# Batch 0 of a sparse-attention kernel with a feed-forward stage: zero products in TensorE's waits, block sums of v as f32 products, another order of the start, an earlier load of w_in

## The chip, the core and the metric

The kernel runs on one core of a Trainium2 chip. The metric is the device time of one execution in microseconds (us), the median of ten runs. The engines are named as the profile names them: PE is TensorE (its weight loads, which overlap products, are PEld), DVE is VectorE, ACT is ScalarE, POOL is GpSimd and SP is SyncE. Each engine works through its own queue in order.

## What is computed

```python
# q, k, v: (4 batches, 8 heads, 768 rows, 64); block 32, window 16
k_sum = k.reshape(B, H, nb, block, D).max(axis=3)
v_sum = v.reshape(B, H, nb, block, D).mean(axis=3)
scores_l = scale * q @ k.T                      # kept where |i - j| < 16
scores_s = scale * q @ k_sum.T + log(block)     # 24 blocks
a = softmax(concat([scores_l, scores_s]))
attn = a @ concat([v, v_sum])
x = attn as (3072 tokens, 512)
h = x @ w_in                                    # 512 x 2048
g = h * clip(h + 3, 0, 6) / 6
out = g @ w_out                                 # 2048 x 512
```

The excerpt shortens the reference to its formulas. Attention makes x, and a feed-forward stage with a hard-swish makes the output of x.

## The kernel before, in words

Heads are taken in pairs, four pairs p in a batch, and each batch is cut in two halves of 384 rows. So there are eight tiles of x, each with four pairs. A tile goes through F1 (hidden products `hp`, 16 groups of 128 columns, four products each, then `r` on ACT and `g` on DVE) and F2 (products `op` with `w_out`, copied to `ot` and stored).

The attention of batch 0 comes first, in an order written out by hand for PE, ACT and DVE (lines 480 to 508). POOL's queue is by hand for the whole kernel. For a pair the steps are:

- `K(0,p)`: sixteen transposes of k into `tp` (L297). ACT copies the lower half of the partitions into `kbd`, DVE the upper half (L306). DVE takes the block maximum `red` (L310) and writes `kst` (L317).
- `Tq(0,p,0)`: sixteen transposes of the first 480 rows of q (L336), which ACT copies into `qT` (L337).
- `S_first(p)`: seven score products in two groups (L345), the exponential on ACT (L348), and the mask on DVE (L349), into `at`.
- `v_first(p)`: `vsum0` (L253 to 267) and `vcast` (L245 to 248). `vcast` writes f32 v to bf16 `vbd`, half on ACT and half on DVE. In `vsum0` the indicator `ind` (128 x 32) sums blocks of 32 rows by an f32 product, for two pairs together. ACT copies the sums out (L263), and DMAs rearrange them into `vs96`, 96 rows of 64 (L266).
- `to_vst(g)`: DVE multiplies these sums by a head mask into `vst` of two pairs (L232).
- `Ss(0,g,0)`: block scores of two pairs (L355), exponential into `asum` (L358).
- `AV(0,p,0)`: products `num` (L381, L383) and `den` (L387 to L397), then on ACT a logarithm and an exponential (L399, L400), and x = num times that on DVE (L401).

v is loaded in f32 by eight DMAs on SP (`load_vf`); k and q come by POOL's queue. Loads of the weights (`load_weights`: w_in in four parts with the late rows of q between, then w_out in four) stand behind `hold_loads`: POOL copies one element of the rearranged sums of pairs 2 and 3, which makes POOL wait for them. w_in part 0 serves hidden groups 0 to 3.

After the hand-made start, the list at the end of the function interleaves F1, F2 and the attention of later batches by slots; a scheduler sets PE's, ACT's and DVE's order there. The remaining rows of batch 0's first half of q (`Tq(0,p,1)`, 288 rows) are transposed from slot 2 on.

PSUM banks in use are two each of `ps_h`, `ps_o`, `ps_s`, and `num` and `den` of `ps_n`.

Of the kernel before, what the change touches and what calls it, by code (L numbers as in the profile page):

```python
# [9 lines left out]
F32 = mybir.dt.float32  # L10
BF16 = mybir.dt.bfloat16
# [5 lines left out]
D = 64  # L17
BLK = 32
KB = 64
HALO = 15  # L20
# [12 lines left out]
def kernel(  # L33
# [145 lines left out]
    def hold_loads(src):  # L179

        nc.gpsimd.tensor_copy(pace[0:src.shape[0], 0:1], src)
# [8 lines left out]
                            channel_multiplier=-1, pattern=[[NB, 4], [0, D]])  # L190
    hmv = [hm4[:, 2 * par:2 * par + 2] for par in range(2)]
    osum = [osum4[:, 2 * par:2 * par + 2] for par in range(2)]
    obd = const.tile([128, 2, D], BF16, tag="obd", name="obd")
    hmk = const.tile([128, 2, NB], BF16, tag="hmk", name="hmk")
    half_c = const.tile([128, 1], F32, tag="half", name="half_c")
    zero = const.tile([128, 1], F32, tag="zero", name="zero")
    nc.vector.memset(zero[:], 0.0)

    def zero_off_diagonal(eng, t):
        w = t.rearrange("p n c -> p (n c)").bitcast(F32).rearrange("p (n c) -> p n c", c=64)  # L200
        for r, c in ((slice(0, 64), slice(32, 64)), (slice(64, 128), slice(0, 32))):
            if eng is nc.scalar:
                eng.copy(w[r, :, c], zero[r].unsqueeze(2).to_broadcast([64, NK, 32]))
            else:
                eng.memset(w[r, :, c], 0.0)


    ind = const.tile([128, 32], F32, tag="ind", name="ind")
    nc.vector.memset(ind[:], 0.0)
    for i in range(4):  # L210
        nc.vector.memset(ind[32 * i:32 * i + 32, 8 * i:8 * i + 1], 1.0)
    for p in range(NP):
        zero_off_diagonal(nc.vector if p < 2 else nc.scalar, kbd[p][:])
    for p in range(2):
# [15 lines left out]
    def to_vst(g, a):  # L230
        for par in range(2):
            nc.vector.tensor_tensor(vst[2 * g + par][:], a.unsqueeze(1).to_broadcast([RS, 2, D]), hmv[par],  # L232
                                    op=ALU.mult)
# [11 lines left out]
    def vcast(p):  # L245
        for j in range(2):
            rows = slice(64 * j, 64 * j + 64)
            (nc.vector.tensor_copy if j else nc.scalar.copy)(vbd[p][rows, :, rows], vf[p][rows])


    vps, vs96 = {}, {}

    def vsum0(p):  # L253
        g, par = p // 2, p % 2
        if par == 0:
            vps[g] = ps_n.tile([128, NK, D // 2], F32, tag=("num", "den")[g], name="vps")
        for h in range(2):
            c = 2 * h + par
            nc.tensor.matmul(vps[g][32 * c:32 * c + 32], ind[:], vf[p][:, :, h * (D // 2):(h + 1) * (D // 2)],  # L259
                             start=True, stop=True)  # L260
        if par == 1:
            a = ld.tile([128, NK, D // 2], F32, tag="vr", name="vs8", bufs=2)
            nc.scalar.copy(a[:], vps[g][:])  # L263
            vs96[g] = work.tile([RS, D], F32, tag="vs96", name="vs96")
            for h in range(2):
                (nc.sync if g == 1 and h == 0 else nc.gpsimd).dma_start(  # L266
                    out=vs96[g][:, h * (D // 2):(h + 1) * (D // 2)], in_=a[64 * h:64 * h + 64:8])


    asum = {}  # L270
# [50 lines left out]
            nc.vector.tensor_tensor(o, red[:].unsqueeze(1).to_broadcast([128, 2, NB]), hmk[:], op=ALU.mult)  # L321

    def Tq(b, p, part=None):
        pool, tag = (ps_h, "h") if b == 0 else (ps_s, "s")
        tp = pool.tile([128, S], BF16, tag=tag, name="tp")
        t, i = qb_t[b, p, part]
        if b >= NLONG:
            for s in range(NT):
                nc.tensor.transpose(tp[:, s * 128:(s + 1) * 128], t[:, s].rearrange("p h d -> p (h d)"), ident[:])
            nc.vector.tensor_copy(qT[p][:, PAD:PAD + S], tp[:])  # L330
            return
        lo, hi, n = cut(part)
        r = (hi - lo) // n
        for s in range(n):
            for j in range(2):
                nc.tensor.transpose(tp[64 * j:64 * j + 64, s * r:(s + 1) * r], t[:, 2 * i + j, s], ident[0:r, 0:r])  # L336
        nc.scalar.copy(qT[p][:, PAD + lo:PAD + hi].rearrange("p (c s) -> p c s", s=n),  # L337
                       tp[:, 0:hi - lo].rearrange("p (s c) -> p c s", s=n))
# [12 lines left out]
    def Ss(b, g, half):  # L351
        sp = ps_s.tile([128, 512], F32, tag="s", name="ss")
        for par in range(2):
            p = 2 * g + par
            nc.tensor.matmul(sp[0:RS, 0:HALF], kst[p][:], qT[p][:, PAD + half * HALF:PAD + (half + 1) * HALF],  # L355
                             start=(par == 0), stop=(par == 1))
        a = work.tile([RS, HALF], BF16, tag="asum", name="asum", bufs=4)
        nc.scalar.activation(a[:], sp[0:RS, 0:HALF], AF.Exp, scale=scl)  # L358
        asum[b, g, half] = a
# [8 lines left out]
        return res  # L368

    xt = {}  # L370

    def AV(b, p, half):
        s = 2 * b + half
        if s not in xt:
            xt[s] = xp.tile([128, NP, HALF], BF16, tag="x", name="x")
        a, asm = at[p], asum[b, p // 2, half]
        alt = b == 0 and p % 2 == half
        pool = ps_o if alt else ps_n
        num = pool.tile([128, HALF], F32, tag="o" if alt else "num", name="num")
        bl = blocks_of(half)  # L380
        nc.tensor.matmul(num[:], vst[p][:].rearrange("p h d -> p (h d)"), asm[:], start=True, stop=False)  # L381
        for i, (t, lo, hi, off) in enumerate(bl):
            nc.tensor.matmul(num[:, lo:hi], vbd[p][:, t], a[:, t, off:off + hi - lo],  # L383
                             start=False, stop=(i == len(bl) - 1))
        den = pool.tile([128, HALF], F32, tag="o" if alt else "den", name="den")
        ones = obd[:].rearrange("p h d -> p (h d)")
        nc.tensor.matmul(den[:], osum[p % 2].rearrange("p h d -> p (h d)"), asm[:], start=True, stop=False)  # L387
        t0, t1 = (0, NK // 2) if half == 0 else (NK // 2, NK)
        d3 = den[:].rearrange("p (n c) -> p n c", c=KB)
        nc.tensor.matmul(d3, ones, a[:, t0:t1, HALO:HALO + KB], start=False, stop=False)  # L390

        if half == 0:
            nc.tensor.matmul(d3[:, :, KB - HALO:], ones, a[:, 1:7, 0:HALO], start=False, stop=False)
            nc.tensor.matmul(d3[:, 1:, 0:HALO], ones, a[:, 0:5, HALO + KB:], start=False, stop=True)  # L394
        else:
            nc.tensor.matmul(d3[:, 0:5, KB - HALO:], ones, a[:, 7:12, 0:HALO], start=False, stop=False)
            nc.tensor.matmul(d3[:, :, 0:HALO], ones, a[:, 5:11, HALO + KB:], start=False, stop=True)  # L397
        lg = work.tile([128, HALF], F32, tag="lg", name="lg")
        nc.scalar.activation(lg[:], den[:], AF.Ln)  # L399
        nc.scalar.activation(lg[:], lg[:], AF.Exp, scale=-1.0)  # L400
        nc.vector.tensor_tensor(xt[s][:, p], num[:], lg[:], op=ALU.mult)  # L401
# [57 lines left out]
    def load_weights():  # L459
        for c in range(2):  # L460
            load_w_in(c)
        load_q(0, 0, 4, 1)
        for c in range(2, 4):
            load_w_in(c)
        for c in range(4):
            load_w_out(c)

    def S_first(p):
        for lo, hi in ((0, 4), (4, NK0)):
            Sl(0, p, lo, hi)  # L470

    def v_first(p):
        vsum0(p)
        vcast(p)
        if p == NP - 1:
            hold_loads(vs96[1][:, 0:1])
            hold_loads(vs96[1][:, D // 2:D // 2 + 1])
            load_weights()

    zero_rest()  # L480
    K(0, 0)
    Tq(0, 0, 0)
    v_first(0)
    for p in range(2, NP):
        zero_off_diagonal(nc.vector, vbd[p])
    S_first(0)
    v_first(1)
    K(0, 1)
    Tq(0, 1, 0)
    S_first(1)  # L490
    nc.vector.tensor_scalar_mul(osum4[:], hm4[:], float(BLK))
    K(0, 2)
    to_vst(0, vs96[0][:])
    Tq(0, 2, 0)
    Ss(0, 0, 0)
    v_first(2)
    v_first(3)
    AV(0, 0, 0)
    K(0, 3)
    Tq(0, 3, 0)  # L500
    S_first(2)
    AV(0, 1, 0)
    S_first(3)
    Ss(0, 1, 0)
    to_vst(1, vs96[1][:])
    AV(0, 2, 0)
    AV(0, 3, 0)
    start.__exit__(None, None, None)

# [56 lines left out]
                 + [(None, NTILE - 1)])  # L566
    for n, (f1, f2) in enumerate(work_list):
        for i in range(NFT):
            if f1 is not None:
                F1(f1, i, f2 is None)  # L570
            if f2 is not None:
                for j in range(3):
                    F2(f2, 3 * i + j, by_ft=f2 == 0)
            for _, f in sorted(plan.pop(16 * n + i, []), key=lambda e: e[0]):
                f()
# [31 lines left out]
```

## Time and profile before

| | before |
|---|---|
| median of 10 runs (lowest, highest) | 261.31 us (260.85, 262.13) |
| the profiled execution's own time | 261.7 us |
| its span, first to last instruction | 259.8 us |
| PE busy | 241.4 us (93%) |
| ACT busy | 167.9 us (65%) |
| DVE busy | 155.0 us (60%) |
| POOL busy | 67.4 us (26%) |
| granted TensorE clock, mean | 0.999 |

The span leaves out 1.9 us of the execution's time that lie around its instructions. By stretches of the span, PE is busy as follows:

| stretch, us | PE busy, us | share |
|---|---|---|
| 0 to 5.4 | 0.00 | 0% |
| 5.4 to 10.5 | 3.57 | 70% |
| 10.5 to 16 | 3.71 | 67% |
| 16 to 20 | 3.44 | 86% |
| 20 to 23 | 3.00 | 100% |
| 23 to 28.2 | 3.70 | 71% |
| 28.2 to 36.3 | 7.30 | 90% |
| 36.3 to 64 | 27.65 | 100% |
| 64 to 128 | 61.02 | 95% |
| 128 to 240 | 111.83 | 100% |

In rows of the profile, `out<-in` gives what an instruction writes and reads; shapes are partitions x elements; `x16` is a count; what stands after `|` is busy time in us and the mean of one in ns, then the engine's idle time before the group with what ended it. In the timeline, the columns are the start in us, the length of the merged stretch, the engine, the line, the operation, and in brackets the idle time before it. A busy PE includes the tail of a product, so the length of a group of products is a little more than its pace times its count.

### The profile page before, as it was taken

Reading aid. Unit: us, or ns where it says so; the run is one execution under the profiler, and the core shown is the slowest. Engines: PE = TensorE matmul, PEld = TensorE weight load, DVE = VectorE, ACT = ScalarE, POOL = GpSimd, SP = SyncE. Lnnn points to the kernel's source line nnn. Section 1 sums busy time; section 2 is a strip of 40 time slices with the busy share of each in tenths; the row PEclk is TensorE's granted clock in tenths of the full one; section 3 lists DMA queues with packets and bytes.
Section 4 is the critical chain, followed back from the end, with each engine's and each line's share of the span. In section 5 each row is a group of like instructions: output and inputs, shape, how many; then the busy total and the mean of one; then the engine's idle time right before and its main releaser. Section 6 shows DMA issues by size and latency. Waiting matters only on the chain.

```text
span 259.8 us, 5035 instructions
## 1 busy us (share of the span) xinstructions
PE 241.4 (93%) x1952; PEld 139.9 (54%) x1952; DVE 155.0 (60%) x357; ACT 167.9 (65%) x326; POOL 67.4 (26%) x101
## 2 busy tenths in 40 slices
PE   1779789999999999798999999999999999999994
PEld 1336456644555556565555555566655555555553
DVE  4877256632578948999884697658544444444400
ACT  8577469833887878869676657766856655555410
POOL 7316500742991112979430400000000000000000
PEclk9999999999999999999999999999999999999999
DMA  6962999899999186999991551101011111101122
GB/s 127 199 119 37 205 204 201 128 231 212 178 202 119 24 256 78 96 81 194 179 134 40 36 68 42 43 1 43 0 40 43 40 40 43 40 0 42 43 81 81
DMA packets 62847, 25.80 MB, mean 99 GB/s; under 512 B 51280, under 2 KB 58728, under 8 KB 62824
## 3 DMA queue, kind: packets, MB, share of 16 engines
q0 software_dynamic: 52848, 17.61, 58.4%
q1 hardware_dynamic: 9976, 7.88, 9.8%
q8 instruction: 15, 0.25, 0.4%
q14 instruction: 8, 0.07, 0.1%
HBM read 31.98 MB, written 6.29 MB: 147 GB/s over the span
## 4 chain that ended last, share of the span: by engine, by line
PE 75%; DVE 10%; DMA 6%; ACT 4%; issue 2%; SPq 1%; POOL 0%; ACTq 0%
PE op L431 29%; PE hp L414 28%; DMA vf<-in_v_dram 3%; PE num L383 3%; PE sl L345 3%; DVE g L418 2%; DMA win<-in_moe_w_in_dram 2%; PE ss L355 2%; PE num L381 2%; PE den L387 2%; PE den L390 2%; DVE red L312 1%; ACT r L417 1%; PE tp L336 1%; PE vps L259 1%
## 5 line engine op out<-in xcount | busy, mean ns | idle before, releaser
L414 PE MATMUL hp<-x,win 128*128 128x384 bf16 x512 | 105.9, 329 | 2.3 <-DVE g L418 1.5
L417 ACT ACTIVATE r<-hp,half_c 128x384 f32<-128x384 f32 x128 | 73.4, 580 | 45.5 <-PE hp L414 43.4
L418 DVE SCALAR_TENSOR_TENSOR g<-r,hp 128x384 bf16<-128x384 f32 x128 | 69.7, 551 | 51.7 <-ACT r L417 51.4
L431 PE MATMUL op<-wout,g 128*128 128x512 bf16 x368 | 98.3, 379 | 0.0
L414 PEld LDWEIGHTS <-win 128*128 128x128 bf16 x512 | 47.8, 98 | 37.6 <-issue 5.7
L431 PEld LDWEIGHTS <-g 128*128 128x128 bf16 x368 | 35.2, 98 | 30.4 <-issue 0.6
L401 DVE TENSOR_TENSOR x<-num,lg 128x384 bf16<-128x384 f32 x32 | 17.7, 554 | 27.4 <-ACT lg L400 25.7
L399 ACT ACTIVATE lg<-den 128x384 f32<-128x384 f32 x32 | 15.7, 492 | 19.3 <-PE den L394 11.7
L120 POOL DMA_DIRECT2D vbd<-in_v_dram x24 | 18.1, 770 | 35.1 <-PE num L383 24.1
L348 ACT ACTIVATE at<-sl 128x376 bf16<-128x376 f32 (+2 forms) x48 | 22.2, 488 | 4.8 <-PE sl L345 4.7
L349 DVE TENSOR_TENSOR at<-at,mask 128x376 bf16<-128x376 bf16 (+2 forms) x48 | 16.3, 348 | 3.5 <-ACT at L348 3.2
L345 PEld LDWEIGHTS <-kbd 128*128 128x128 bf16 x192 | 12.5, 103 | 9.1 <-DVE kbd L306 3.0
L400 ACT ACTIVATE lg<-lg 128x384 f32<-128x384 f32 x32 | 16.8, 526 | 0.9
L435 ACT COPY ot<-op 128x512 f32<-128x512 f32 x23 | 13.2, 585 | 5.9 <-PE op L431 5.7
L383 PEld LDWEIGHTS <-vbd 128*128 128x128 bf16 x224 | 13.9, 104 | 5.6 <-issue 2.4
L345 PE MATMUL sl<-qT,kbd 128*128 128x94 bf16 x192 | 15.4, 216 | 1.6 <-DVE kbd L306 1.6
L383 PE MATMUL num<-at,vbd 128*128 128x94 bf16 (+2 forms) x224 | 15.1, 208 | 0.0
L113 POOL DMA_DIRECT2D qb<-in_q_dram x16 | 13.6, 880 | 3.7 <-DMA vr<-in_v_dram 1.9
L113 POOL DMA_DIRECT2D kb<-in_k_dram x16 | 13.6, 872 | 0.4 <-PE hp L414 0.4
L381 PE MATMUL num<-asum,vst 96*128 96x384 bf16 x32 | 11.2, 350 | 0.6 <-ACT vs L263 0.6
L390 PE MATMUL den<-at,obd 128*128 128x384 bf16 x32 | 11.4, 357 | 0.0
L387 PE MATMUL den<-asum,osum 96*128 96x384 bf16 x32 | 11.0, 345 | 0.0
(87 smaller groups left out, 215.7 us busy)
## 6 DMA issues: line engine op xcount, KB each, us to landing
out_dram<-ot SPq DMA_DIRECT2D x23, 256.0 KB, 2.0
vr<-in_v_dram POOLq DMA_DIRECT2D x6, 768.0 KB, 9.3
vbd<-in_v_dram POOLq DMA_DIRECT2D x24, 96.0 KB, 4.5
win<-in_moe_w_in_dram POOLq DMA_DIRECT2D x4, 512.0 KB, 9.2
wout<-in_moe_w_out_dram POOLq DMA_DIRECT2D x4, 512.0 KB, 17.5
vf<-in_v_dram SPq DMA_DIRECT2D x8, 192.0 KB, 7.5
kb<-in_k_dram POOLq DMA_DIRECT2D x16, 96.0 KB, 5.1
qb<-in_q_dram POOLq DMA_DIRECT2D x16, 96.0 KB, 5.0
```

The costliest lines, as they stand in the source:

```text
L113: nc.gpsimd.dma_start(out=t[:, :, j], in_=src[b, 2 * p + j].rearrange("(s p) d -> p s d", p=128))
L120: nc.gpsimd.dma_start(out=vall[rows, p, lo:hi, rows], in_=v[b, 2 * p + j].rearrange("(n k) d -> k n d", k=KB)[:, lo:hi])
L345: nc.tensor.matmul(sp[:, i * WIN:(i + 1) * WIN], kbd[p][:, t], qT[p][:, PAD - HALO + t * KB:PAD - HALO + t * KB + WIN], start=True, stop=True)
L348: nc.scalar.activation(a, sp[:, 0:n * WIN].rearrange("p (n c) -> p n c", c=WIN), AF.Exp, scale=scl)
L383: nc.tensor.matmul(num[:, lo:hi], vbd[p][:, t], a[:, t, off:off + hi - lo], start=False, stop=(i == len(bl) - 1))
L390: nc.tensor.matmul(d3, ones, a[:, t0:t1, HALO:HALO + KB], start=False, stop=False)
L400: nc.scalar.activation(lg[:], lg[:], AF.Exp, scale=-1.0)
L401: nc.vector.tensor_tensor(xt[s][:, p], num[:], lg[:], op=ALU.mult)
L414: nc.tensor.matmul(hp[:], w_in_sb[:, kt, ft * 128:(ft + 1) * 128], xt[t][:, kt], start=(kt == 0), stop=(kt == NP - 1))
L417: nc.scalar.activation(r[:], hp[:], AF.Relu, bias=half_c[:], scale=1.0 / 6.0)
L418: last_g[0] = nc.vector.scalar_tensor_tensor(gt[t][:, ft], r[:], 1.0, hp[:], op0=ALU.min, op1=ALU.mult)
L431: nc.tensor.matmul(op[:], gt[t][:, ft, ts * 128:(ts + 1) * 128], w_out_sb[:, ft], start=(ft == 0), stop=(ft == NFT - 1))
```

## The change

1. An all-zero bf16 tile `idle` (128 x 512). Ten products of it into a bank of `ps_n` stand first in PE's queue, and four more between the transposes of k and q of pair 0.
2. `vsum0` sums v in another way: twelve f32 products per pair, one for each 64 rows, with a 96-column slice of a wider indicator. They accumulate over two pairs in a bank of 96 x 64, which `to_vst` reads directly. The copy, the rearranging DMAs and `vs96` go.
3. The order of the start is another one. `K(0,1)` comes before the first scores of pair 0; `K` and `Tq` of pair 3 come before the first outputs; casts of v of pairs 2 and 3 come later.
4. The hold ahead of the weight loads reads `kbd` of pair 2, where it read the sums of pairs 2 and 3.
5. The zeros off the diagonal of `vbd` for pairs 2 and 3 are written by POOL, not by DVE.
6. `AV(0,p,0)` and the transposes of q use other PSUM banks, and F1 of tile 0 is scheduled after the last `den` product of pair 2.

```diff
+    for p in range(2, NP):
+        w = vbd[p].rearrange("p n c -> p (n c)").bitcast(F32).rearrange("p (n c) -> p n c", c=64)
+        nc.gpsimd.memset(w[0:64, :, 32:64], 0.0)
+        nc.gpsimd.memset(w[64:128, :, 0:32], 0.0)
...
+    idle = const.tile([128, 512], BF16, tag="idle", name="idle")
+    nc.vector.memset(idle[:], 0.0)
...
+    def busy(t, n):
+
+        for _ in range(n):
+            nc.tensor.matmul(t[:], idle[:, 0:128], idle[:], start=True, stop=True)
+
+    busy_n = ps_n.tile([128, 512], F32, tag="den", name="busy_n")
+    busy(busy_n, 10)
...
-    ind = const.tile([128, 32], F32, tag="ind", name="ind")
+    ZI = 2 * NB + NK - 1
+    ind = const.tile([128, ZI + RS], F32, tag="ind", name="ind")
...
-            nc.tensor.matmul(vps[g][32 * c:32 * c + 32], ind[:], vf[p][:, :, h * (D // 2):(h + 1) * (D // 2)],
-                             start=True, stop=True)
...
+        for n in range(lo, hi):
+            o = ZI - par * 2 * NB - n
+            nc.tensor.matmul(vps[g][:], ind[:, o:o + RS], vf[p][:, n], start=(par == 0 and n == 0),
+                             stop=(par == 1 and n == NK - 1))
...
     K(0, 0)
+    busy(busy_n, 4)
     Tq(0, 0, 0)
-    v_first(0)
-    for p in range(2, NP):
-        zero_off_diagonal(nc.vector, vbd[p])
+    vsum0(0)
+    vcast(0)
+    K(0, 1)
     S_first(0)
-    v_first(1)
-    K(0, 1)
+    vsum0(1, 0, NK // 2)
     Tq(0, 1, 0)
+    vsum0(1, NK // 2, NK)
+    vcast(1)
+    nc.vector.tensor_scalar_mul(osum4[:], hm4[:], float(BLK))
+    to_vst(0, vps[0][:])
+    K(0, 2)
+    hold_loads(kbd[2][0:64, 0, 0:1])
+    load_weights()
     S_first(1)
-    nc.vector.tensor_scalar_mul(osum4[:], hm4[:], float(BLK))
-    K(0, 2)
-    to_vst(0, vs96[0][:])
     Tq(0, 2, 0)
-    Ss(0, 0, 0)
-    v_first(2)
-    v_first(3)
-    AV(0, 0, 0)
     K(0, 3)
     Tq(0, 3, 0)
+    Ss(0, 0, 0)
+    vsum0(2)
+    vcast(2)
     S_first(2)
-    AV(0, 1, 0)
+    AV(0, 0, 0)
+    vcast(3)
+    vsum0(3)
+    to_vst(1, vps[1][:])
     S_first(3)
     Ss(0, 1, 0)
-    to_vst(1, vs96[1][:])
+    AV(0, 1, 0)
     AV(0, 2, 0)
+    first_x = last_av[0]
     AV(0, 3, 0)
...
-            if f1 is not None:
+            if f1 == 0:
+                with tc.issue_after(first_x.ins):
+                    F1(0, i, True)
+            elif f1 is not None:
                 F1(f1, i, f2 is None)
```

More of the change, by code (lines that the diff above doesn't have):

```diff
@@ L205, in zero_off_diagonal @@
                 eng.memset(w[r, :, c], 0.0)
-    ind = const.tile([128, 32], F32, tag="ind", name="ind")
+    ZI = 2 * NB + NK - 1
+    ind = const.tile([128, ZI + RS], F32, tag="ind", name="ind")
     nc.vector.memset(ind[:], 0.0)
     for i in range(4):
-        nc.vector.memset(ind[32 * i:32 * i + 32, 8 * i:8 * i + 1], 1.0)
+        nc.vector.memset(ind[32 * i:32 * i + 32, ZI + NK * i:ZI + NK * i + 1], 1.0)
     for p in range(NP):
@@ L248, in vcast, with vsum0 @@
             (nc.vector.tensor_copy if j else nc.scalar.copy)(vbd[p][rows, :, rows], vf[p][rows])
-    vps, vs96 = {}, {}
-    def vsum0(p):
+    vps = {}
+    def vsum0(p, lo=0, hi=NK):
         g, par = p // 2, p % 2
[L255 to L259, printed above, removed]
-                             start=True, stop=True)
[L261 to L267, printed above, removed]
+        if par == 0 and lo == 0:
+            vps[g] = ps_n.tile([RS, D], F32, tag=("num", "den")[g], name="vps")
+        for n in range(lo, hi):
+            o = ZI - par * 2 * NB - n
+            nc.tensor.matmul(vps[g][:], ind[:, o:o + RS], vf[p][:, n], start=(par == 0 and n == 0),
+                             stop=(par == 1 and n == NK - 1))
     asum = {}
@@ L323, in Tq @@
     def Tq(b, p, part=None):
-        pool, tag = (ps_h, "h") if b == 0 else (ps_s, "s")
+        pool, tag = (ps_s, "s") if b else (ps_o, "o") if part == 0 else (ps_h, "h")
         tp = pool.tile([128, S], BF16, tag=tag, name="tp")
@@ L370 @@
     xt = {}
+    last_av = [None]
     def AV(b, p, half):
@@ L376, in AV @@
         a, asm = at[p], asum[b, p // 2, half]
-        alt = b == 0 and p % 2 == half
-        pool = ps_o if alt else ps_n
-        num = pool.tile([128, HALF], F32, tag="o" if alt else "num", name="num")
+        pool, tags = (ps_n, ("num", "den")) if b or p == 2 or half and p % 2 == 0 else (ps_h, "hh") if p == 1 and half == 0 else (ps_o, "oo")
+        num = pool.tile([128, HALF], F32, tag=tags[0], name="num")
         bl = blocks_of(half)
@@ L384, in AV @@
                              start=False, stop=(i == len(bl) - 1))
-        den = pool.tile([128, HALF], F32, tag="o" if alt else "den", name="den")
+        den = pool.tile([128, HALF], F32, tag=tags[1], name="den")
         ones = obd[:].rearrange("p h d -> p (h d)")
@@ L393, in AV @@
             nc.tensor.matmul(d3[:, :, KB - HALO:], ones, a[:, 1:7, 0:HALO], start=False, stop=False)
-            nc.tensor.matmul(d3[:, 1:, 0:HALO], ones, a[:, 0:5, HALO + KB:], start=False, stop=True)
+            last_av[0] = nc.tensor.matmul(d3[:, 1:, 0:HALO], ones, a[:, 0:5, HALO + KB:], start=False, stop=True)
         else:
@@ L470, in S_first @@
             Sl(0, p, lo, hi)
[L472 to L478, printed above, removed]
     zero_rest()
     K(0, 0)
+    busy(busy_n, 4)
     Tq(0, 0, 0)
-    v_first(0)
-    for p in range(2, NP):
-        zero_off_diagonal(nc.vector, vbd[p])
+    vsum0(0)
+    vcast(0)
+    K(0, 1)
     S_first(0)
-    v_first(1)
-    K(0, 1)
+    vsum0(1, 0, NK // 2)
     Tq(0, 1, 0)
+    vsum0(1, NK // 2, NK)
[5 more added lines that the diff above has]
+    load_weights()
     S_first(1)
-    nc.vector.tensor_scalar_mul(osum4[:], hm4[:], float(BLK))
-    K(0, 2)
-    to_vst(0, vs96[0][:])
     Tq(0, 2, 0)
-    Ss(0, 0, 0)
-    v_first(2)
-    v_first(3)
-    AV(0, 0, 0)
     K(0, 3)
     Tq(0, 3, 0)
+    Ss(0, 0, 0)
+    vsum0(2)
+    vcast(2)
     S_first(2)
-    AV(0, 1, 0)
+    AV(0, 0, 0)
+    vcast(3)
+    vsum0(3)
+    to_vst(1, vps[1][:])
     S_first(3)
     Ss(0, 1, 0)
-    to_vst(1, vs96[1][:])
+    AV(0, 1, 0)
     AV(0, 2, 0)
+    first_x = last_av[0]
     AV(0, 3, 0)
```

## The prediction, made before the changed kernel ran

> **What bounds the kernel now.** I read four views in this order: the page's shares by engine, the chain of waits over the first 70 us, the timeline of the start, and the groups by shape of the first 36 us. The page puts TensorE (PE) at 93% of the span; from 36.30 us on, PE waits for another engine for 3.4 us in all. What can move is the start, so the question is when the last output tile of batch 0, x of pair 3, is written. From the chain of waits (start, length, what):
>
> ```profile
> 3.00 7.50 DMA vf<-in_v_dram
> ...
> 12.17 0.48 ACT vs L263
> ...
> 20.00 1.87 DMA vs<-vs
> ...
> 22.68 5.50 DMA win<-in_moe_w_in_dram
> 28.18 0.05 issue
> 28.23 1.46 PE hp L414 x4
> 29.69 0.32 PE num L381
> ...
> 35.70 0.56 DVE g L418
> 36.26 0.04 issue
> 36.30 0.43 PE tp L336 x16
> ```
>
> The end is set by v arriving, block sums, a small transfer that rearranges them (vs), a hold that lets w_in go only then (22.68), 5.50 us for w_in part 0, four hidden-layer products, and behind these in PE's queue the outputs (num, den) of pairs 2 and 3. x of pair 3 is written at 34.54; the first later transposes (tp) run 1.76 us after that.
>
> w_in is not late alone. The block sums of pairs 2 and 3 are multiplied out (vst) only at 27.42 to 27.90, so with w_in early and nothing else changed, pair 2 could begin at 27.9 instead of 29.69: 1.8 us. More must come from the engines. The second thing to see is PE's pace:
>
> ```profile
> 32.67 2.87 PE L414 MATMUL hp<-x,win 128*128 128x384 bf16 x12
> ...
> 33.62 0.15 PEld L414 LDWEIGHTS <-win 128*128 128x128 bf16 x1 [0.17 <-issue]
> 33.94 1.20 PEld L414 LDWEIGHTS <-win 128*128 128x128 bf16 x7 [0.17 <-issue]
> ```
>
> Weight loads of one and the same product start 0.32 us apart until 33.94, then 0.17 us apart. The granted clock is 1.00 throughout, so it doesn't show this; durations do. All of PE's work before 33.9 runs at half pace. Third, from the groups by shape (busy us and mean ns of one, then idle before it), the old sums and DVE's load:
>
> ```profile
> L259 PE MATMUL vps<-vf,ind 128*32 128x384 f32 x16 | 4.5, 846 | 0.9 <-DMA vf<-in_v_dram 0.9
> ...
> L306 DVE COPY kbd<-tp 64x768 bf16<-64x768 bf16 x4 | 3.8, 960 | 3.9 <-ACT kbd L306 3.8
> L310 DVE TENSOR_REDUCE red<-tp 128x24 bf16<-128x768 bf16 x4 | 3.8, 958 | 0.1
> ...
> L401 DVE TENSOR_TENSOR x<-num,lg 128x384 bf16<-128x384 f32 x4 | 2.2, 558 | 7.3 <-ACT lg L400 7.3
> ```
>
> DVE (VectorE) is idle 7.3 us before the outputs: it has room now, which the change uses up.
>
> **The change part by part.** DMA landings don't move: issue plus time to landing gives k of pair 1 at 9.7, k of pairs 2/3 at 13.1, q of 2/3 at 14.6, v of pairs 0 to 3 at 7.2, 10.5, 15.7, 17.2.
>
> *Block sums.* Gone: eight products of 384 columns (16 records, 4.5 us), two ACT copies of 0.48, four small transfers (4.3 us landing, three of POOL's issues of 0.61), one hold. Added: 48 f32 products, weights 96 columns, moving 64. The old ones took two records each and 4 records in 1.49 us for two products side by side, so 0.64 us a record for 384 columns, or 0.107 us for 64 at half pace, 0.053 at full. A weight load may hide or not: an f32 load of 32 columns lasted 0.14, so the ends per record are 0.107 to 0.2 slow, 0.053 to 0.13 full. I take 0.15 and 0.08, between: nearest row 0.076 pitch for 94-column bf16 products whose loads hide. That is 96 records: 7.7 us at full pace, 14.4 at half.
>
> *Products of zeros.* 14 products of 512 columns. At 384 columns in 0.32, one costs 0.43 at half pace: ten from 1.1 (after two memsets) to 5.4, where k of pair 0 lands (5.4): hidden. Four more stand before the q transposes of pair 0: 6.1 to 7.8 at half pace, 0.8 us past q's landing at 7.0. Cover: what follows needs k of pair 1 at 9.7. Without cover they cost 0.8.
>
> *Does it warm PE?* Row: PE had no gap from 28.23 to 33.94, so 5.7 us passed before the pace doubled. [...] The trace agrees as far as it can: PE was also busy from 20.0 to 23.77, of which 1.4 us were transposes, and stayed slow. [...] By the row, counting anew after the transposes of pair 0, full pace at 12 to 14: 29.2 to 29.8. I take 8.
>
> *Order.* K(0,1) ahead of the first scores, K and q transposes of pair 3 ahead of the first outputs; zeros of vbd for pairs 2/3 from DVE (4 x 0.378) to POOL, some 0.46 each by hm's memset of 0.31 for 256 columns, 8.9 to 10.8, needed after 17: hidden. DVE's two larger early memsets (0.2) lie in its 2.4 us of idle before 7.17.
>
> *w_in.* The hold now reads kbd of pair 2, which ACT copies after k's landing: 13.1, transposes, ACT's queue, 14.5. So w_in is issued at 15.1 instead of 22.68; its data would flow some 2 us later, when v (17.2) is in. Landing 20.6 to 22. The whole list on POOL moves 7.6 us earlier: the late part of q from 34.1 to 26.5, w_in parts 1 to 3 from 30.7, 36.1, 38.6 to 23.1, 28.5, 31.0; their uses (36.3, 36.8, 41.1, 44.2) move by 7.0 at my forecast, so slack stays. The w_out parts (41.2 to 48.8) have nine us.
>
> *No hidden-layer product before pair 2's outputs*: takes the 1.46 us out of PE's queue there; behind it nothing waits any more for w_in.
>
> **The sum.** With PE fast, DVE becomes the bound. Its first copy for pair 1 can start at about 11.6 (sums of pair 0 to 10.2, k transposes 0.5, ACT copy 0.79). From then without a gap: 0.96 + 0.96 + 0.28 (kbd, red, kst of pair 1), masks 0.57, cast 0.56, osum 0.28, vst 0.48 = 4.1; pair 2: 2.20 + masks 0.57 = 2.8; pair 3: 2.2; cast 0.56, masks 0.57, x of pair 0 0.56, cast 0.56, vst 0.48 = 2.7. Together 11.8, so vst of pairs 2/3 is there at 23.4. Then num and den of pair 2 at full pace (1.0, as they ran from 45.53 to 46.55): 24.5; ACT's logarithm and exponential for pairs 2 and 3, four of 0.52: 26.6; x of pair 3, 0.56: **27.2**. ACT is near its limit too (16.8 us of work from 6.3: 23.1 with no wait), so no much better order hides behind DVE. The same summing of the old queues, at half pace, gives 34.75 where the trace has 34.54, so I trust it to some tenths.
>
> Saved 34.54 - 27.2 = 7.3; then hidden products that must wait for x of pair 3 (its bank is also shared by the second of them) make the handover about 2.1 instead of 1.76: -0.3. All later queues have the same order. So 261.7 (the profiled execution; its span is 259.8) - 7.0 = 254.7. That execution lies 0.4 above the median 261.31: forecast **254.3**.
>
> **Rivals.**
> *Late warming* (full pace at 12 to 14; or the 96 records cost 0.13 each at full pace): x of pair 3 at 29.2 to 31.0, time 256.3 to 258. For it: 5.7 us in the trace and the transposes. Against: PE's queue has almost no gap from 1.1 to 12 now.
> *PE stays slow and the new sums are its bound*: PE's work after 7.8 without sums is 4 x 0.48 + 3 x 0.66 + 4 x 0.55 + 2 x 0.64 + 4 x 1.6 = 13.8, plus 96 records: at 0.15, 14.4, so 36.0, and 2.3 for the last log, exponential and x: 38.3, or 3.8 later than now, **265**; at 0.187 it is 268. It decides above 0.11 a record. For it: all PE work before 33.9 was slow, though often 70 to 86% busy. Against: a PE so bound has no gaps, which is what made it fast at 33.9.
> *The transfers undo it*: w_in's data share the queue with v of pair 3; if v of pairs 2 and 3 land 2 us later, x of pair 3 is at 28.2 (pair 2's sums stand ahead of the first output): 255.4. Speaks against: the 2 us between issue and flow.
>
> **How the numbers follow.** Forecast 0.57; late warming or dear records 0.20; transfers 0.10; slow PE 0.10, of which some ends near no change; the rest 0.03. The best end is DVE starting at 10.6, k-bound: 252.8. The range takes that and late warming's upper part: 252.6 to 258.4. Within 0.2% is what cannot be told from no change. Faster 0.87, same 0.03, slower 0.10.
>
> **What would show it.** Right: weight loads and 128x384 products at the short spacing before 10 us; DVE without gaps from about 12 to 23; vs transfers gone; w_in issued near 15; PE waiting for vst or ACT, not w_in; the first late transposes near 29.3. Wrong: products of zeros but 0.32 spacing after 12; the sums' records above 0.1 at full pace; hp or tp waiting for win or qb after 27; time after 36 us not equal to before's.

## The result, and the profile after

| | before | changed |
|---|---|---|
| median, us | 261.48 (32 runs) | 254.78 (9 runs, 254.29 to 258.73) |
| profiled execution, its time and span | 261.7, 259.8 | 255.62, 253.5 |
| w_in issued | 22.68 | 15.04 |
| vst of pairs 2 and 3 complete | 27.90 | 23.57 |
| x of pair 3 complete | 34.54 | 28.29 |
| first late transposes | 36.30 | 29.93 |

The ratio is 0.9746 (95% interval 0.9731 to 0.976): 6.7 us saved. In a later group of runs the changed kernel took 254.88. Ratios leave out runs more than 1.5% above a kernel's shortest, here one of nine (258.73) and below most runs of one kernel, which are therefore given in full.

The late transposes begin 6.37 us earlier and the span is 6.3 us shorter, so the whole gain is in the start and nothing is given back later. The chain of waits of the changed kernel (start, length, what):

```profile
6.47 10.63 DMA vf<-in_v_dram
17.09 0.14 issue
17.23 2.22 PE vps L274 x24
...
20.61 2.06 PE vps L274 x24
22.67 0.18 PE sl L353 x4
22.88 0.49 ACT at L356
...
23.41 0.48 PE ss L363 x2
23.89 0.17 PE num L389
...
24.79 0.50 ACT lg L407
...
25.74 0.48 ACT lg L407
...
26.67 0.48 ACT lg L407
27.18 0.53 ACT lg L408
27.73 0.57 DVE x L409
28.30 0.04 issue
28.34 0.34 PE hp L422
```

Neither the small transfer nor w_in is in it any more. What is left is v of pair 2, the f32 sums of pairs 2 and 3, the scores behind them, the outputs of pair 1 (num, from 23.89), and then three pairs of logarithms and exponentials on ACT. `vst` is not in it. In the timeline, the rows that answer to PE's pace:

```profile
1.27 4.38 PE L208 MATMUL busy_n<-idle 128*128 128x512 bf16 x10 [1.27 <-DVE zero L203]
...
5.58 0.53 PE L305 MATMUL tp<-ident,kb 96*64 96x96 bf16 x16
...
6.04 1.04 PE L208 MATMUL busy_n<-idle 128*128 128x512 bf16 x4
...
7.83 2.25 PE L274 MATMUL vps<-vf,ind 128*96 128x64 f32 x24
```

The same k transposes in the profile of before:

```profile
5.46 0.85 PE L297 MATMUL tp<-ident,kb 96*64 96x96 bf16 x16 [5.46 <-DMA kb<-in_k_dram]
```

They took 0.85 us there and take 0.53 now, four products of zeros 1.04 instead of 4 x 0.43, and 24 records of the new sums 2.25, so 0.09 each with the tail off. PE is at full pace from 5.6 us on. DVE, in its own timeline, has no gap from 11.44 to 24.04; then it waits for ACT:

```profile
20.24 0.28 DVE L325 TENSOR_TENSOR kst<-red,hmk 128x24 bf16<-128x24 bf16 x2
20.55 0.85 DVE L263 CAST vbd<-vf 64x768 bf16<-64x768 f32 x1
21.42 0.57 DVE L357 TENSOR_TENSOR at<-at,mask 128x376 bf16<-128x376 bf16 x2
21.91 0.55 DVE L409 TENSOR_TENSOR x<-num,lg 128x384 bf16<-128x384 f32 x1
22.49 0.56 DVE L263 CAST vbd<-vf 64x768 bf16<-64x768 f32 x1
23.08 0.49 DVE L247 TENSOR_TENSOR vst<-vps,hm 96x128 bf16<-96x128 f32 x2
...
25.87 0.56 DVE L409 TENSOR_TENSOR x<-num,lg 128x384 bf16<-128x384 f32 x1 [1.82 <-ACT lg L408]
```

### The profile page after: what moved, and what is told of

It is laid out like the page before. It is cut to its first block, busy times and chain, and to the rows that moved or that the text cites. A ratio compares the mean times of both kernels' runs of the same rounds, so it can differ in the third digit from the quotient of the medians.

```text
span 253.5 us, 5214 instructions
## 1 busy us (share of the span) xinstructions
PE 242.9 (96%) x2046; PEld 144.5 (57%) x2046; DVE 154.3 (61%) x354; ACT 166.9 (66%) x324; POOL 67.2 (27%) x101
## 4 chain that ended last, share of the span: by engine, by line
PE 75%; DVE 11%; DMA 5%; ACT 4%; SPq 2%; issue 2%; ACTq 0%
PE op L439 29%; PE hp L422 27%; DMA vf<-in_v_dram 4%; PE num L391 3%; DVE g L426 3%; PE sl L353 3%; SPq L129 2%; PE ss L363 2%; PE num L389 2%; PE den L395 2%; PE vps L274 2%; PE den L398 2%; DVE red L320 2%; ACT r L425 1%; DVE x L409 1%
## 5 line engine op out<-in xcount | busy, mean ns | idle before, releaser
L422 PE MATMUL hp<-x,win 128*128 128x384 bf16 x512 | 104.7, 326 | 1.9 <-DVE g L426 1.5
L439 PEld LDWEIGHTS <-g 128*128 128x128 bf16 x368 | 35.2, 98 | 30.4 <-issue 0.6
L407 ACT ACTIVATE lg<-den 128x384 f32<-128x384 f32 x32 | 15.7, 491 | 14.3 <-PE den L405 7.3
L408 ACT ACTIVATE lg<-lg 128x384 f32<-128x384 f32 x32 | 16.8, 526 | 0.9
L391 PEld LDWEIGHTS <-vbd 128*128 128x128 bf16 x224 | 12.9, 98 | 5.1 <-issue 1.6
L353 PEld LDWEIGHTS <-kbd 128*128 128x128 bf16 x192 | 11.8, 98 | 6.1 <-issue 1.0
L353 PE MATMUL sl<-qT,kbd 128*128 128x94 bf16 x192 | 14.4, 206 | 0.0
L391 PE MATMUL num<-at,vbd 128*128 128x94 bf16 (+2 forms) x224 | 14.1, 199 | 0.0
L398 PE MATMUL den<-at,obd 128*128 128x384 bf16 x32 | 10.7, 333 | 0.0
L389 PE MATMUL num<-asum,vst 96*128 96x384 bf16 x32 | 10.4, 326 | 0.1
L395 PE MATMUL den<-asum,osum 96*128 96x384 bf16 x32 | 10.4, 325 | 0.0
## 6 DMA issues: line engine op xcount, KB each, us to landing
wout<-in_moe_w_out_dram POOLq DMA_DIRECT2D x4, 512.0 KB, 16.8
```

What stands on the lines that cost most here:

```text
L353: nc.tensor.matmul(sp[:, i * WIN:(i + 1) * WIN], kbd[p][:, t], qT[p][:, PAD - HALO + t * KB:PAD - HALO + t * KB + WIN], start=True, stop=True)
L422: nc.tensor.matmul(hp[:], w_in_sb[:, kt, ft * 128:(ft + 1) * 128], xt[t][:, kt], start=(kt == 0), stop=(kt == NP - 1))
L439: nc.tensor.matmul(op[:], gt[t][:, ft, ts * 128:(ts + 1) * 128], w_out_sb[:, ft], start=(ft == 0), stop=(ft == NFT - 1))
```

## The experiments

Times of the kernel before beside them: 261.43, 261.40 and 261.71 in the three groups of runs. "First late tp" is where the transposes of q's late rows begin, as in the table above.

| kernel | median, us | pace of PE | w_in issued | first late tp |
|---|---|---|---|---|
| changed | 254.78 | full from 5.6 | 15.04 | 29.93 |
| changed, no zero products | 263.24 | half until about 29 | 19.79 | 37.72 |
| changed, first ten only (long runs) | 263 | full to 8, half to about 29 | 19.79 | 37.67 |
| changed, narrow f32 fill | 263.98 | half until about 29 | 20.56 | 38.31 |
| before, zero products | 261.66 | full 6 to 13, lost twice | 23.73 | 36.98 |
| before, zero products in the waits too | 260.12 | full from about 7 | 23.25 | 34.92 |
| changed, late w_in | 258.38 | full | 22.59 | 33.03 |
| changed, old sums | 273.57 | full to 15, then lost | 14.66 | 48.19 |
| changed, old sums, late w_in | 266.95 | lost twice | 29.33 | 42.14 |

**Is it the zero products? The changed kernel without them.**

```diff
-    busy(busy_n, 10)
...
-    busy(busy_n, 4)
```

> The changed kernel without its 14 products of zeros. My theory (the fill brings PE to full pace before 6 us): without it PE starts slow, the f32 records of pair 0 cost 0.11 to 0.15 us instead of 0.09, and full pace comes near 12 us at the earliest, from the unbroken sums after the q transposes: x of pair 3 some 2 us later, so 256.5 to 257.5 against 254.8. Rival 1 (the denser new order warms PE by itself, the fill is idle work): 254.8 within 0.4. Rival 2 (nothing else would warm it in the start): PE-bound, 262 or more.

Measured: 263.24 us (ratio 1.0066, 1.0037 to 1.0096). My number was too small by 6 us; rival 2 is right. The timeline:

```profile
7.81 4.10 PE L272 MATMUL vps<-vf,ind 128*96 128x64 f32 x24
11.84 0.85 PE L303 MATMUL tp<-ident,kb 96*64 96x96 bf16 x16
...
21.92 4.00 PE L272 MATMUL vps<-vf,ind 128*96 128x64 f32 x24
...
27.85 2.62 PE L272 MATMUL vps<-vf,ind 128*96 128x64 f32 x24
30.30 0.46 PE L351 MATMUL sl<-qT,kbd 128*128 128x94 bf16 x7
```

PE has no gap from 10 to 29 us, and the sums stay at 0.165 us a record. Two stretches of them last about 4 us unbroken. Full pace comes only within the last 24 records (2.62 us, between the 4.00 of half pace and the 2.22 of full), after the first wide bf16 outputs (26.27 to 27.85). So here being busy in the profile was not enough to raise the pace. With PE slow, k of pair 2 is transposed late too, and w_in goes at 19.79: the pace moves the loads as well.

**Which products raise it? A fill of narrow f32 products.**

```diff
-    idle = const.tile([128, 512], BF16, tag="idle", name="idle")
+    idle = const.tile([128, 96], F32, tag="idle", name="idle")
...
-            nc.tensor.matmul(t[:], idle[:, 0:128], idle[:], start=True, stop=True)
+            nc.tensor.matmul(t[0:96, 0:64], idle[:], idle[:, 0:64], start=True, stop=True)
...
-    busy(busy_n, 10)
+    busy(busy_n, 13)
...
-    busy(busy_n, 4)
+    busy(busy_n, 5)
```

> The changed kernel with its fill made of f32 products of 64 columns with 96-column weights (13 and 5 in place of 10 and 4, about the same 4.3 us at the slow pace, PE just as busy in the profile). Theory (what raises the pace is wide products that keep the array streaming; the narrow f32 ones that ran from 10 to 29 us without the fill did not): as without a fill, 262.5 to 264. Rival (any unbroken 4 us of products raises it, and only the transposes between stood in the way): 254.8 within 0.5.

Measured: 263.98 us (1.0064 to 1.0121), as the theory said. Its timeline:

```profile
1.10 4.42 PE L208 MATMUL busy_n<-idle 128*96 128x64 f32 x26 [1.10 <-DVE zero L203]
5.45 0.85 PE L305 MATMUL tp<-ident,kb 96*64 96x96 bf16 x16
```

PE is as long busy as with the wide fill (4.42 against 4.38 us), and the transposes behind it take 0.85 instead of 0.53. One profile would not settle it: the changed kernel with the first ten only, the next run, comes out short in three executions of ten and long in seven. But all six runs are long (263.35 to 264.51), and so are the ten without a fill (262.54 to 264.29). So between these two fills the kind of product decides. The two fills differ in width, in type, in the columns of their weights and in the number of weight loads; no run separates these.

**Are the four later ones needed?**

```diff
-    busy(busy_n, 4)
```

> The changed kernel without the four later products of zeros. Full pace stood at 5.6 us already, and PE then waits 1.0 us for q of pair 0 instead of filling it. Theory (ten raise the pace, small waits don't lower it): 254.8 within 0.4. Rival (the four are needed, because transposes and narrow f32 products count little): the pace falls back between 8 and 15 us, 258 or more.

Measured: ten runs, three at 254.14 to 254.91 and seven at 262.75 to 263.31. The rival is right seven times in ten. The profiled execution, one of the long ones, by stretches (us, each engine's busy time and count, granted clock, DMA share, GB/s):

```profile
5.40:7.00 1.60, 0.53 (x16) 0.40 (x16) 0.00 (x0) 1.45 (x3) 1.40 (x5) 1.00 1.31 215
7.00:9.00 2.00, 1.45 (x24) 1.41 (x24) 1.75 (x2) 1.13 (x3) 1.74 (x6) 0.77 1.30 197
9.00:11.00 2.00, 2.00 (x15) 2.00 (x15) 1.02 (x4) 0.45 (x1) 1.75 (x4) 0.50 1.23 200
```

Between 5.4 and 7.0 PE does 0.53 us of transposes and nothing else. At 8 the granted clock falls to half (0.50 from 10 to 25), and the sums that follow do not bring it back. Six of the seven long runs have a mean granted clock of 0.96, which is some 21 us at half (an estimate: 0.04 of 261 us, doubled), as in this profile; the seventh reads 0.998, and what happened in it is open. The same kernel comes out 8 us apart from run to run. No short run of it was profiled, so what saved it is not shown.

**The zero products alone, in the old kernel.** The diff adds the tile, the function and both calls of the change.

> The old kernel with the 14 products of zeros only. My theory: PE runs at full pace from 6 us, so the outputs of pairs 2 and 3 take 1.0 us each instead of 1.6, but they still stand behind w_in part 0, which is issued at most 1 us earlier than 22.7: time 258 to 259. Rival (PE falls back to the slow pace in the old order's waits, which are longer): 261.3 within 0.4, with weight loads 0.32 us apart at 30 us. Rival (w_in didn't matter, only the pace did): 255 to 256.

Measured: 261.66 us (0.9979 to 1.0033), no change. My theory is wrong and the first rival right. By stretches:

```profile
10.00:15.00 5.00, 2.30 (x43) 1.42 (x43) 4.28 (x9) 2.45 (x5) 1.22 (x2) 0.77 1.23 212
15.00:20.00 5.00, 5.00 (x52) 2.17 (x51) 4.43 (x14) 3.46 (x7) 0.00 (x0) 0.55 0.39 57
...
25.00:30.00 5.00, 1.10 (x5) 0.40 (x5) 1.62 (x7) 0.71 (x2) 5.00 (x8) 0.64 1.06 160
30.00:35.00 5.00, 4.87 (x35) 3.05 (x34) 0.77 (x2) 2.03 (x4) 0.50 (x1) 0.68 1.25 204
```

PE is busy 2.30 of the 5 us from 10 on, and the clock falls. It recovers near 19.5 (0.55 from 15 to 20, 1.00 from 20 to 25) and is lost again in the wait for w_in (0.64 from 25 to 30):

```profile
29.36 1.46 PE L424 MATMUL hp<-x,win 128*128 128x384 bf16 x4 [3.90 <-DMA win<-in_moe_w_in_dram]
```

**The old kernel with the waits filled too.**

```diff
     Tq(0, 1, 0)
+    busy(ps_o.tile([128, 512], F32, tag="o", name="busy_o"), 8)
...
     Ss(0, 1, 0)
+    busy(ps_o.tile([128, 512], F32, tag="o", name="busy_o"), 14)
```

> The old kernel with the 14 products of zeros and 22 more in the two waits where the pace was lost: 8 behind the q transposes of pair 1 (2 us of wait near 12 us), 14 behind the block scores of pairs 2 and 3 (the wait for w_in near 26 us). Theory 1 (fill alone did nothing because the old order's waits undid it): full pace from 6 us to the end, outputs of pairs 2 and 3 take 1.0 us instead of 1.6, but w_in still lands near 28: 259 to 260. Rival (pace is worth nothing in the old order, w_in and the vs transfers set everything): 261.5 within 0.4. Rival (w_in comes earlier too once PE is fast): below 258.

Measured: 260.12 us (ratio 0.9914 to 0.9975), 0.1 above the range of theory 1. From about 7 us the pace holds (no granted clock under 1.00 to 50 us, and every later product short), `num` and `den` of all four pairs are done at 29.6, and then:

```profile
30.07 2.77 PE L424 MATMUL hp<-x,win 128*128 128x384 bf16 x16 [0.49 <-DMA win<-in_moe_w_in_dram]
34.92 0.43 PE L346 MATMUL tp<-ident,qb 36*64 36x36 bf16 x16 [2.08 <-DMA qb<-in_q_dram]
```

Full pace without the early loads, in the old order, is worth 1.3 us: late q rows, behind w_in in POOL's queue, become the wait.

**The changed kernel with w_in late.**

```diff
-    hold_loads(kbd[2][0:64, 0, 0:1])
-    load_weights()
...
     vcast(3)
+    hold_loads(vbd[3][0:64, 0, 0:1])
+    load_weights()
```

> The changed kernel with the hold on ACT's half of the cast of v of pair 3, so w_in is issued near 22.6 us instead of 15.0. Two questions. Is the early load needed: my theory says that F1 then waits for w_in (28.3) and the first late transposes for the late rows of q (near 33 instead of 29.9): 257.5 to 258.5. Rival (DVE and ACT are the only bound): below 255.5. And why v of pair 2 landed at 17.1 instead of the 15.7 of before: if w_in's early issue takes part of v's transfers, v of pairs 2 and 3 lands near 15.7 and 17.2 again here and x of pair 3 comes up to 1 us earlier than 28.3; if it is not w_in, v lands at 17.1 and 18.1 here too.

Measured: 258.38 us, 3.6 above the changed kernel, as the theory said. F1 waits for w_in, then the transposes for q:

```profile
28.09 2.77 PE L422 MATMUL hp<-x,win 128*128 128x384 bf16 x16 [1.64 <-DMA win<-in_moe_w_in_dram]
...
33.03 0.43 PE L344 MATMUL tp<-ident,qb 36*64 36x36 bf16 x16 [0.59 <-DMA qb<-in_q_dram]
```

The second question: the later transfer for v of pair 2, issued at 6.0 here, took 11.0 us to land (17.0), with w_in still unissued. With w_in at 14.66 (the next run) it landed at 15.7, as before the change. So v lands between 15.7 and 17.1 from one execution to the next, and w_in doesn't set that.

**The new order with the old sums.** Indicator, `vsum0` and `vs96` of the old kernel, the rest as changed.

> The changed kernel with the old block sums (two wide f32 products a pair, ACT copy, rearranging transfers), in the new order, with the fill and the early hold. PE saves some 6 us of the 8.6 us of small f32 products, but vst waits for copies and transfers of 2 to 4.4 us that stand in POOL's queue among the weight loads. My theory (the direct sums matter by cutting these transfers): vst of pairs 2 and 3 comes at 25 or later, 256 to 258. Rival (PE's share of the new sums is a loss of its own): vst at 23.5 or before, S_first of pairs 2 and 3 earlier, 254.5 or less.

Measured: 273.57 us (1.0412 to 1.0481), worse than the theory by far, for a reason that I had named and not priced:

```profile
41.45 0.50 PE L395 MATMUL num<-asum,vst 96*128 96x384 bf16 x1 [15.34 <-DVE vst L246]
```

POOL's half of the sums of pairs 2 and 3 was issued at 24.2 and landed 16.8 us later: it stood behind 8 parts of weights that POOL had issued before it, and the quickest of these transfers in this run took 4.6. To take that away:

```diff
-    hold_loads(kbd[2][0:64, 0, 0:1])
-    load_weights()
...
     vsum0(3)
+    hold_loads(vs96[1][:, 0:1])
+    hold_loads(vs96[1][:, D // 2:D // 2 + 1])
+    load_weights()
```

> The new order and the fill, with the old block sums and the old hold on their transfers. It takes away what spoilt the run with old sums and early w_in, where the vs transfers stood behind the weights for 15 us. Theory: PE has fewer products between 8 and 15 us, loses the pace near 15 again, and w_in is issued near 25: 263 to 265. Rival (the new order is worth it without the new sums): 258 or less.

Measured: 266.95 us (1.0128 to 1.0251), two above the range. Three waits stand out: one for DVE, whose queue waits for the sums of pairs 0 and 1, one for `vst` of pairs 2 and 3, and one for w_in:

```profile
20.16 0.73 PE L359 MATMUL sl<-qT,kbd 128*128 128x94 bf16 x7 [3.31 <-DVE kbd L320]
...
28.93 0.34 PE L395 MATMUL num<-asum,vst 96*128 96x384 bf16 x1 [2.51 <-DVE vst L246]
...
34.84 6.27 PE L428 MATMUL hp<-x,win 128*128 128x384 bf16 x20 [3.77 <-DMA win<-in_moe_w_in_dram]
```

By stretches:

```profile
20.00:25.00 5.00, 4.05 (x30) 2.19 (x31) 4.77 (x12) 3.24 (x8) 0.06 (x1) 0.66 0.00 0
...
30.00:35.00 5.00, 1.23 (x13) 0.76 (x12) 1.14 (x3) 2.03 (x4) 5.00 (x8) 0.54 0.88 135
...
40.00:45.00 5.00, 3.81 (x54) 2.24 (x53) 1.49 (x4) 2.51 (x6) 0.00 (x0) 0.94 1.24 206
```

The pace falls at 20.2, at the end of the first wait, is back at 23.6, falls again at 30.4, between the second wait and the third, and stays at half to 40.6; so the 20 hidden products take 6.27 us. So the new order without the new sums is a loss of 5.5 us. The direct sums do two things for it: they need no transfer, so the weights can go first, and with them PE is busy 4.78 of the 5 us from 10 to 15.

**Is there more in the order?** Two variants beside the changed kernel, on one chip.

> The changed kernel once more, beside the two below on one chip: 254.3 to 255.3, with v of pair 2 landing anywhere from 15.7 to 17.1 us in the profiled execution.

> The changed kernel with the tail of its start in another order: block scores of pairs 0/1 before the q transposes of pair 2, first scores of pair 2 ahead of its sums, those of pair 3 ahead of the first outputs, casts of pair 3 with those of pair 2. In the changed kernel PE waits 0.9 us for v of pair 2 with the scores of pair 2 queued behind, and the outputs of pair 1 start only at 23.7 because the scores of pair 3 stand behind its sums. Theory (v's landing and the sums behind it set x of pair 3): x of pair 3 near 27.5 instead of 28.3, 253.8 to 254.3. Rival (DVE's work alone sets it, vst of pairs 2 and 3 at 23.5 in any order): same as the changed kernel within 0.3.

> The changed kernel with three more products of zeros behind the block scores of pairs 0 and 1, in the 0.9 us that PE waits for v of pair 2. They end before v lands, so nothing should be later: 254.3 to 255.3. If the one run of the changed kernel at 258.7 had lost the pace in that wait, no such run should come here; the rival is that the products run past v's landing when it is early (15.7) and cost up to 0.6.

```diff
# the other order
     S_first(1)
+    Ss(0, 0, 0)
     Tq(0, 2, 0)
     K(0, 3)
     Tq(0, 3, 0)
-    Ss(0, 0, 0)
+    S_first(2)
     vsum0(2)
     vcast(2)
-    S_first(2)
-    AV(0, 0, 0)
     vcast(3)
+    S_first(3)
+    AV(0, 0, 0)
     vsum0(3)
     to_vst(1, vps[1][:])
-    S_first(3)
# more fill
     Ss(0, 0, 0)
+    busy(ps_n.tile([128, 512], F32, tag="den", name="busy_2"), 3)
     vsum0(2)
```

Measured: the changed kernel 254.88, the other order 255.12, more fill 255.48 (0.2 above its range); the intervals of the ratios overlap (0.9716 to 0.9764, 0.9727 to 0.9769, 0.9745 to 0.9802). Neither is an improvement. In the changed kernel's second profile v of pair 2 was not waited for, x of pair 3 stood at 27.72 and the late transposes at 29.34. From the other order's timeline:

```profile
22.89 0.33 PE L389 MATMUL num<-asum,vst 96*128 96x384 bf16 x1
...
23.30 0.47 DVE L247 TENSOR_TENSOR vst<-vps,hm 96x128 bf16<-96x128 f32 x2
...
23.95 0.49 ACT L407 ACTIVATE lg<-den 128x384 f32<-128x384 f32 x1 [0.37 <-PE den L402]
...
26.89 0.56 DVE L409 TENSOR_TENSOR x<-num,lg 128x384 bf16<-128x384 f32 x1 [0.38 <-ACT lg L408]
```

The rival's number holds, but its reason does not. `vst` of pairs 2 and 3 was complete later than in the second profile of the changed kernel (23.77 against 23.21), and x of pair 3 still came sooner (27.45 against 27.72). In all four profiles of the three kernels x of pair 3 is complete 3.50 us after ACT begins the logarithm of pair 1 (24.79 to 28.29, 24.21 to 27.72, 23.95 to 27.45, 24.32 to 27.82). So ACT's three pairs of logarithms and exponentials set the end, from the moment that PE has done the outputs of pair 1, and PE has no gap ahead of these in the other order from 15.75 on.

Whether the run of 258.73 lost the pace near v of pair 2 stays open. Its mean granted clock of 0.985, against 0.997 to 1.00 in the other runs, says that it lost it somewhere, for some 6 to 8 us at half (an estimate: 0.015 of its span of 256.7 us, doubled, is 7.7, of which the others have up to 1.5). No run came out so long among the five with more fill, nor among the four without.

## Why the prediction was right, step by step

- **The total.** Forecast 254.3, measured 254.78 (and 254.88). Forecast saving at the late transposes 7.0, measured 6.37 and 6.96 in two profiles. The pace, the early loads and the end of the rearranging transfers did what the sum has them do; the path of its last 4 us is another one (below).
- **The pace.** Taken at full from 8 us, measured from 5.6. It differs by profile: with the first ten only they took 3.99 us against 4.38, so the pace rose within them, and in the old kernel with zero products the k transposes behind the ten took 0.63 us, between the 0.85 of half pace and the 0.53 of full. In the table's seven profiles with the wide ten, q's transposes or the sums behind them run at full pace by 7.9 us. So the 5.7 us of the old trace, counted anew after the transposes, put it too late. No trace of before and no run shows the 8 itself; what the runs show is 5.6 in the changed kernel and 7.9 at the latest.
- **The cost of the new sums.** Taken 0.08 a record, measured 0.09: 8.6 us in all instead of 7.7. At half pace taken 0.15, measured 0.165.
- **w_in.** Issued at 15.04 against a forecast of 15.1. The claim that slack stays holds: PE waits neither for win nor for late q.
- **DVE as the bound.** The sum put vst of pairs 2 and 3 at 23.4; it was complete at 23.57, after a queue without a gap, though one cast in it took 0.85 instead of 0.56. But it is not the wait that ended last. PE was still to do the outputs of pair 1, from 23.73 to 24.59, before those of pair 2, and the chain goes through these and ACT. That the end came near is in part luck.
- **The outputs** are where it was off: x of pair 3 at 28.29 instead of 27.2, so the sum was off by 1.1 where I trusted it to some tenths. The sum had pair 1's outputs done before vst, with two pairs of logarithms behind it. In the trace they stand behind the block scores of pairs 2 and 3, so ACT had three pairs behind it, at 0.94 us a pair. In the first profile v of pair 2 also landed at 17.1 instead of 15.7. Without that wait (the second profile) x of pair 3 is at 27.72, so v's landing is worth 0.57 of the 1.1 us and the order of the outputs the rest. The first profile has the place and size of the transfers rival (x at 28.2), but not its cause: v landed as late with w_in unissued, and SP issues v where POOL issues w_in. The handover gave 0.46 back: 1.64 us instead of 2.1.
- **The slow-PE rival.** The run without a fill is what it described, at 263.2 where it said 265. But my argument against it was wrong. I held that a PE without gaps raises its own pace; 19 us without gaps did not. The chance of 0.10 was too low for a change that hangs on four zero products: without these, seven runs in ten fall into it.

## What to carry to other kernels

When a stage's products run at twice their later length, look for it in durations before counting on busy time, and fill the waits with wide products ahead of the first real ones. Then check that the stage behind is dense enough to keep the pace: the fill was worth 8.5 us with the dense order and early loads, nothing in the old order, and 1.3 us there with its waits filled too. The parts hold each other up. Taking the fill out of the change costs 8.5 us, the early load 3.6, the new sums 12.2 (with the old hold) or 18.8. What the new order, the new sums or the early load would give alone in the old kernel, and what the moved zeros, the other banks and the later F1 are worth, no run shows.

## What the runs showed of the hardware that I had not expected

- Where the pace was lost, PE stayed at half for several us. A stretch's mean granted clock tells when (an estimate that takes each moment as 1.00 or 0.50, the two readings of most stretches): 0.77 from 10 to 15 is 54% at full, so the fall was at 12.7. In the old kernel with the zero products the clock falls at 12.7, is back at 19.5, falls at 26.4 and is back at 33.2, about 6.8 us apart each time. In the new order with old sums and late w_in, 0.66 from 20 to 25 is 3.4 us at half, and the second time at half lasts from 30.4 to 40.6, 10.2 us. With the first ten only (0.79 from 5.4 to 10, 0.65 from 25 to 30) it is half from 8.1 to 28.5, 20.4 us. What sets these lengths is not shown.
- Wide zero products raised the pace: ten of them, 3.99 to 4.38 us with the tail, stand ahead of full pace by 7.9 us in all seven profiles of the table that have them. The narrow f32 fill of 4.42 us did not. What share of the time must be products, and whether transposes count, no run shows.
- In the changed kernel the narrow f32 sums, at 0.09 us a record, follow the fill from 7.83 on and the pace stays. At half pace they ran 4 us unbroken twice without a fill (4.10 and 4.00 us) and twice with the first ten only (4.00 and 3.99), and did not raise it.
- The granted clock doesn't show the slow start. It reads 1.00 from 5 to 29 us in the run without a fill, where every product is slow. It reads 0.50 only where a pace once reached is lost, as from 10 to 25 us with the first ten only.
- A DVE cast of 64x768 took 0.85 us (20.55) while POOL was issuing loads of w_out (18.72 to 21.74), and 0.56 at the same place in the run with late w_in, where POOL was idle. An earlier one took 0.69 beside POOL's memsets, one of which took 0.72 instead of 0.41. In the changed kernel's second profile the cast at that place took 0.56 under the same issues, and POOL's four issues of w_out 3.13 instead of 3.02. So now the one and now the other is longer; the cause isn't shown.
